# One 128x128 mask, `u` as a row, small fill matmuls, one unit's decay factors by DMA, and every order and bank anew in a RWKV-6 + FFN kernel

## The chip, the cores and the metric

The kernel runs on one core of a Trainium2 chip. The metric is the device time of one execution in microseconds (us); the median of 3 executions is given. TensorE is called PE, VectorE DVE, ScalarE ACT, GpSimd POOL and SyncE SP, as the profile does.

## The reference

Two parts follow each other. The first is a linear recurrence with a 48x48 state for each of 4 batches and 8 heads, over 768 steps; the second is four matrix products with one elementwise product among them.

```python
batch, n_heads, seq, head_dim = (4, 8, 768, 48)
n_tokens, d_model, d_ff = (3072, 384, 1024)
for t in range(S):
    cur = np.einsum('bhd,bhe->bhde', u[None] * kt, vt)
    y[:, :, t] = np.einsum('bhd,bhde->bhe', rt, state + cur)
    state = wt[:, :, :, None] * state + np.einsum('bhd,bhe->bhde', kt, vt)
x = y.transpose(0, 2, 1, 3).reshape(B * S, H * D)
a = x @ w1
b = x @ w2
h = a * b @ w3
return (h @ w_out).astype(np.float32)
```

All inputs and the output are float32; the matrix products of the kernel are in bfloat16.

## The kernel before

Time is cut into 6 chunks of 128 steps. A unit is one chunk of one batch (units 0 and 1) or of two batches (units 2 to 12), all 8 heads; there are 13 units. A step is named by its kind and its unit (`m_4_0`: unit 4, first of its two batches). Each unit has these steps.

- Loads `win`, `kin`, `rin`, `vin` (line 329; unit 0's `k`, `r`, `v` come as float32 into the tiles `wide`, line 320, and `kc`, `rc`, `vc` cast them, line 324).
- `ln` (402, ACT) is the logarithm of the decays; `cs` (414, PE) sums it over the chunk with the triangular matrix `LT`, and in the same step 4 matmuls of one column per batch (419) make the chunk's total decay, of which `pc` (426, ACT) takes the exponential. `ne`, `iw`, `e`, `et` (433, 472, 480, 457, ACT) are further exponentials; `KRk`, `rw`, `KRr`, `rk`, `ruk`, `dg`, `dv` (438, 476, 484, 518, 522, 528, 537) are the products with them, with `u` (tile `u_bc`) in `ruk`. `dv` holds the diagonal term.
- `k` and `r` are transposed on PE (`trk`, `trr`, `trw`, 510, 495, 463) and evicted (`trke`, `trre`, `KRw`), or by DMA on SP's queue (`dtk`, `dtr`, 504, 489).
- `m` (549, PE) is the 128x128 product within the chunk. It is masked to the strictly earlier steps: `msk` (568, DVE) multiplies it out of PSUM by the tile `mask`; where (unit, batch) stands in POOL_MASK, `mcp` (555, ACT) copies it and `maff` masks the copy, by a product (561, DVE) or an affine_select (563, POOL).
- `ys`, `yi` (584, 594, PE) form the output; `yb` (612, DVE) adds `dv`. For a unit in Y_PE, PE adds it (`yd`, 603) and ACT copies (`ybc`, 609). `yt` and `xT` (631, 635), or the DMA transpose `dty` (621), bring it into the layout of the FFN.
- `kv` (647, PE), `T` and `S` (655, 663) and `Sb` (668) carry the state to the next chunk.

The FFN: for each row block `fi` of w3, `wt` transposes it on PE (365), `w3Te` evicts it (369), `wm` multiplies it by w_out (374) and `w34e` evicts (379): so w3 and w_out become one matrix `w34`, whose product is done once. Then each unit has groups `a` and `b` (688, PE), `asb` (693, ACT), `abT` (698, DVE), the product `o` (704, PE), `osb` (709) and the store `st` (714, SP). The weights come in pieces: `w3_0` to `w3_3`, `wo`, and two halves each of w1 and w2.

`warm(at, n)` issues n matmuls of a tile of zeros (302) that nobody reads. They stand in the order where PE would have nothing else to do.

The order of all steps on all engines is written out by hand in `ORDER`, as name@engine; each engine runs its own steps strictly in that order and waits on semaphores for the others. SP, ACT and POOL also issue the DMAs that stand in their order: a DMA behind a waiting step waits too. `BANKS` gives each PSUM user its bank or banks, and each evicted tile its buffer (`sa`, `so`, `M`).

## Time and profile before

| | |
|---|---|
| median of 3 executions | 171.32 us (171.07 to 171.39) |
| the profiled execution: its own time | 171.16 us |
| the profiled execution: span of its instructions | 169.4 us |
| DVE, ACT and POOL busy | 134.1, 89.5 and 86.2 us |
| HBM read and written | 27.98 and 4.72 MB |

All times in rows are microseconds from the start of the span, unless marked ns. A row of a group reads: line, engine, operation, tiles out<-in, form, count | busy time, mean ns of one | idle time just before and what ended it. A matmul's own duration holds its passage through the array: matmuls follow each other faster than that. A row with a window gives, for each engine, its busy time in the window, then the granted clock of PE, and the DMA's share and rate.

```profile
DVE  0568889786789999999999999997799867556260
ACT  3166575258947789689855986611632042330511
POOL 7899874894773838994049607294072023000000
DMA  3999999999999999999959999959949944603313
```

These are 40 equal slices of the span, each with its busy share in tenths.

### The profile page before, as it was taken

The page shows a single profiled execution, that of the slowest core. Times are in us where ns is not written, and L with a number is a line of the kernel's source. Part 1 is how long each engine was busy: PE and PEld are TensorE (multiplying, and loading weights), DVE is VectorE, ACT ScalarE, POOL GpSimd, SP SyncE. Part 2 cuts the span into 40 slices and gives each one's busy share as a digit, 9 for nine tenths or more (in the row PEclk, how much of TensorE's full clock was granted, in tenths as well). Part 3 has the DMA queues.
Part 4 walks back from the last instruction along what each step waited for, and adds up shares of the span by engine and source line. Part 5 has one row for each costly group of instructions (what it writes and reads, how often), then busy time and mean ns, then how long its engine had stood idle before and what let it go on. Part 6 is the DMA issues. An engine that isn't in the chain of part 4 may idle for free.

```text
span 169.4 us, 4733 instructions
## 1 busy us (share of the span) xinstructions
PE 162.6 (96%) x1998; PEld 122.0 (72%) x1998; DVE 134.1 (79%) x221; ACT 89.5 (53%) x151; POOL 86.2 (51%) x83
## 2 busy tenths in 40 slices
...
DVE  0568889786789999999999999997799867556260
ACT  3166575258947789689855986611632042330511
POOL 7899874894773838994049607294072023000000
...
DMA  3999999999999999999959999959949944603313
GB/s 80 212 205 182 146 198 189 206 215 153 183 203 217 175 173 167 172 149 174 194 106 90 174 203 236 164 49 109 135 109 141 157 87 109 165 4 95 137 58 130
DMA packets 98837, 25.63 MB, mean 151 GB/s; under 512 B 90880, under 2 KB 96640, under 8 KB 98816
## 3 DMA queue, kind: packets, MB, share of 16 engines
...
HBM read 27.98 MB, written 4.72 MB: 193 GB/s over the span
## 4 chain that ended last, share of the span: by engine, by line
PE 73%; DVE 11%; DMA 7%; ACT 4%; issue 2%; POOL 1%; SPq 0%; DVEq 0%; ACTq 0%
PE banks L688 28%; PE banks L704 13%; PE banks L302 10%; PE banks L374 6%; DMA vin<-in_v_dram 5%; PE banks L549 3%; DVE abT L698 3%; PE banks L594 2%; PE banks L414 2%; PE banks L510 2%; PE banks L365 1%; DMA out_dram<-osb 1%; DVE dg L528 1%; ACT a_sb L693 1%; PE banks L647 1%
## 5 line engine op out<-in xcount | busy, mean ns | idle before, releaser
L688 PE MATMUL banks<-xT,w_bf 128*128 128x256 bf16 (+1 forms) x624 | 69.7, 264 | 0.5 <-DMA xT<-yb 0.4
L688 PEld LDWEIGHTS <-w_bf 128*128 128x128 bf16 x624 | 55.2, 98 | 7.8 <-issue 1.0
L693 ACT COPY a_sb<-banks 128x512 f32<-128x512 f32 x48 | 27.4, 594 | 27.8 <-PE banks L688 22.5
L698 DVE TENSOR_TENSOR abT<-a_sb,banks 128x512 bf16<-128x512 f32 x48 | 31.6, 681 | 10.4 <-PE banks L688 6.9
L704 PE MATMUL banks<-w,abT 128*128 128x384 bf16 x192 | 34.5, 326 | 0.1
L704 PEld LDWEIGHTS <-abT 128*128 128x128 bf16 x192 | 18.1, 98 | 10.7
L568 DVE TENSOR_TENSOR Mbf<-banks,mask 128x1024 bf16<-128x1024 f32 x17 | 20.4, 1219 | 1.6 <-PE banks L549 1.3
L302 PE MATMUL banks<-zeros 128*128 128x512 bf16 x66 | 19.9, 431 | 1.4 <-DVE zeros L243 1.3
L537 POOL TENSOR_TENSOR dv<-vin,dg 128x768 bf16<-128x768 bf16 x9 | 13.3, 1482 | 15.5 <-DMA vin<-in_v_dram 8.7
L709 ACT COPY osb<-banks 128x384 f32<-128x384 f32 x13 | 6.3, 482 | 21.7 <-PE banks L704 9.2
L329 POOL DMA_DIRECT2D win<-in_w_dram x13 | 15.0, 1157 | 1.1 <-POOLq L748 0.8
L329 POOL DMA_DIRECT2D rin<-in_r_dram x12 | 13.8, 1152 | 2.8 <-DMA w_bf<-in_moe_w_dram 2.5
L402 ACT ACTIVATE lw<-win 128x768 bf16<-128x768 f32 (+1 forms) x13 | 10.5, 811 | 8.7 <-DMA win<-in_w_dram 8.7
L329 POOL DMA_DIRECT2D vin<-in_v_dram x12 | 13.9, 1160 | 2.3 <-DMA w_bf<-in_moe_w_dram 0.9
L329 POOL DMA_DIRECT2D kin<-in_k_dram x12 | 13.8, 1153 | 1.7 <-issue 0.7
L612 DVE TENSOR_TENSOR yb<-banks,dv 128x768 bf16<-128x768 f32 (+1 forms) x12 | 11.1, 921 | 4.4 <-issue 1.8
L302 PEld LDWEIGHTS <-zeros 128*128 128x128 bf16 x66 | 6.5, 108 | 8.2 <-issue 3.8
L433 ACT ACTIVATE NEt<-banks 128x768 bf16<-128x768 f32 (+1 forms) x13 | 9.9, 765 | 3.6 <-PE banks L414 3.6
L663 POOL TENSOR_TENSOR Sst<-Tst,pc 128x384 f32<-128x384 f32 x4 | 3.7, 934 | 15.7 <-DVE Tst L655 15.6
L374 PE MATMUL banks<-wo_bf,w3T 128*128 128x384 bf16 x64 | 11.7, 325 | 0.0
L528 DVE TENSOR_REDUCE dg<-ruk 128x16 f32<-128x768 bf16 (+1 forms) x13 | 11.5, 881 | 0.0
L594 PEld LDWEIGHTS <-Mbf 128*128 128x128 bf16 x192 | 7.8, 96 | 2.5 <-issue 1.1
...
## 6 DMA issues: line engine op xcount, KB each, us to landing
out_dram<-osb SPq DMA_DIRECT2D x24, 192.0 KB, 2.1
win<-in_w_dram POOLq DMA_DIRECT2D x11, 384.0 KB, 9.8
kin<-in_k_dram POOLq DMA_DIRECT2D x11, 192.0 KB, 7.8
rin<-in_r_dram POOLq DMA_DIRECT2D x11, 192.0 KB, 8.4
vin<-in_v_dram POOLq DMA_DIRECT2D x11, 192.0 KB, 8.7
...
w_bf<-in_moe_w_dram POOLq DMA_DIRECT2D x4, 384.0 KB, 12.3
wo_bf<-in_moe_w_out_dram POOLq DMA_DIRECT2D x1, 768.0 KB, 13.5
```

Source lines behind the costliest of these rows:

```text
L302: nc.tensor.matmul(banks[:, at, :], lhsT=zeros[:, :C], rhs=zeros, start=True, stop=True)
L329: QUEUE[eng].dma_start(dst, src)
L374: nc.tensor.matmul(one(f"wm{fi}")[:, :DM], lhsT=w3T[fi % 2][:, gi, :], rhs=wo_bf[:, gi, :], start=(gi == 0), stop=(gi == FI - 1))
L528: nc.vector.reduce_sum(dgs, ruks, axis=AX.X)
L537: e.tensor_mul(dvs, vv, dgs[:, :, None].to_broadcast([C, bh, D]))
L568: nc.vector.tensor_mul(Mbf[bank[f"M{t}_{b}"]], mview(), mask.rearrange("s (j q) t -> s j q t", j=2))
L594: nc.tensor.matmul(o[:, h % 2, b, h // 2, :], lhsT=M[:, h % 2, h // 2, :], rhs=vv[:, b * H + h, :], start=(not c and b == 0 and h < 2), st ...
L612: nc.vector.tensor_add(ybs.rearrange("t b (q e d) -> t e (b q) d", e=2, d=D), yview().rearrange("t e (x d) -> t e x d", d=D), dvs.rearrang ...
L688: nc.tensor.matmul(o[:, f, :], lhsT=wt[:, di, fi * P:(fi + 1) * P], rhs=x[:, di, :T], start=(di == 0), stop=(di == DI - 1))
L693: copier(eng)(a_sb[bank[f"sa{t}_{g}"]], one(f"a{t}_{g}"))
L698: nc.vector.tensor_mul(ab[:, g * per:(g + 1) * per, :T], sa.rearrange("p (f t) -> p f t", t=T), one(f"b{t}_{g}").rearrange("p (f t) -> p f ...
L704: nc.tensor.matmul(one(f"o{t}_{b}")[:, :DM], lhsT=ab[:, fi, b * C:(b + 1) * C], rhs=w34[:, fi, :], start=(fi == 0), stop=(fi == FI - 1))
```

## The change

- `mask` becomes one 128x128 tile, `LT - I128` (DVE), which `msk` and `maff` read through a broadcast; its memset and its affine_select over 1024 columns go.
- `u` is loaded as one row of 384 numbers. One matmul with a row of ones (`ub`) spreads it over the partitions and ACT evicts it (`ue`).
- `warm` counts in quarters: n stands for n pieces of 128 columns, four of them to a matmul. The sum over all calls was 66 matmuls of 512 columns and is 144 pieces, so 36 such matmuls.
- The one-column matmuls become a step of their own (`cc`). Unit 10 has none: `px` (ACT) takes the exponential of the last rows of `cs`, and the DMA `pd` (SP) brings its last row to the partitions.
- `wide` and `u_f` lie inside the last two `abT` tiles; there are 4 `a_sb` buffers for 3.
- POOL_MASK has 4 members for 7, Y_PE has units 0 and 1. Unit 0's loads and `win_1` are issued by SP and ACT; before, `win_0` and `win_1` were POOL's.
- `ORDER` and `BANKS` are new throughout, engines included: `dv_6`, for one, goes to ACT, where it is 16 instructions, one for each of the unit's 2x8 head blocks.
- `DEPTH` is empty and `BLOCKS` has one unit each, so the code with them does what it did.

```diff
-N_X = 4
-N_ASB = 3
-N_AB = 8
+N_X = {2: 4}
+N_ASB = 4
+N_AB = {2: 8}
...
+DEPTH = {}
+BLOCKS = [(0,), (1,), (2,), (3,), (4,), (5,), (6,), (7,), (8,), (9,), (10,), (11,), (12,)]
+ROW_PC = {10}
...
-POOL_MASK = {(2, 0), (2, 1), (3, 0), (4, 0), (6, 1), (7, 1), (8, 1)}
-Y_PE = {1}
+POOL_MASK = {(2, 0), (4, 1), (7, 1), (9, 1)}
+Y_PE = {0, 1}
 BANKS = """
...
 ORDER = """
-table@ACT zeros@DVE u@SP win_0@POOL kin_0@SP rin_0@SP win_1@POOL vin_0@SP rin_1@POOL win_3@POOL kc_0@DVE padlw@DVE
-padet@DVE ones@DVE kin_1@POOL mask1@DVE LT@POOL win_2@POOL ln_0@ACT rc_0@DVE rk_0@DVE warm0@18 cs_0@PE padr@DVE
-kin_2@POOL padkr@DVE ln_1@ACT uc@ACT warm1@6 csT_1@PE w3_0@POOL pc_0@ACT cs_1@PE ruk_0@DVE et_1@ACT ne_0@ACT
-vin_1@POOL pc_1@ACT I128@POOL mask@POOL warm3@9 trw_1@PE csT_0@PE trw_0@PE ln_3@ACT kin_3@POOL ne_1@ACT warm4@3
-csT_3@PE KRk_1@DVE KRk_0@DVE rin_3@POOL rk_1@DVE warm6@2 trk_0@PE vc_0@DVE trk_1@PE KRw_1@DVE trke_0@ACT dg_0@DVE
-rin_2@POOL et_0@ACT et_3@ACT KRw_0@DVE ruk_1@DVE w3_1@POOL warm7@8 m_0_0@PE trke_1@DVE ln_2@ACT cs_3@PE msk_0_0@DVE
-wo@POOL kv_0@PE cs_2@PE vin_3@POOL m_1_0@PE pc_2@ACT ne_2@ACT msk_1_0@DVE warm4@2 wt_0_0@PE w3_2@POOL pc_3@ACT
-wt_1_0@PE ne_3@ACT wt_0_1@PE dg_1@DVE vin_2@POOL kv_1@PE csT_2@PE S_0@DVE dv_0@DVE yi_1_0@PE et_2@ACT dv_1@DVE
-win_4@POOL S_1@DVE warm7@3 yd_1@PE KRk_3@DVE ybc_1@ACT KRk_2@DVE warm7@2 trk_3@PE w3Te_0@ACT win_5@POOL Sb_0@DVE
-yt_1@PE yi_0_0@PE wt_1_1@PE Sb_1@ACT yb_0@DVE trw_3@PE w3Te_1@ACT trke_3@DVE w1_1@POOL warm1@1 trw_2@PE KRw_3@DVE
-trk_2@PE KRw_2@DVE warm4@1 m_3_1@PE rk_3@DVE warm7@1 m_3_0@PE trke_2@DVE mcp_3_0@ACT rin_4@POOL ruk_3@DVE warm7@4
-m_2_0@PE wt_2_0@PE maff_3_0@DVE mcp_2_0@ACT ys_3@PE wt_2_1@PE msk_3_1@DVE xT_1@ACT maff_2_0@POOL warm0@1 wt_3_0@PE
-warm1@1 wt_3_1@PE dg_3@DVE m_2_1@PE yt_0@PE mcp_2_1@ACT rk_2@DVE kin_4@POOL warm4@3 wm_0@PE ruk_2@DVE maff_2_1@POOL
-yi_3_0@PE w3Te_2@DVE wm_1@PE w34e_0@DVE dv_3@POOL dg_2@DVE yi_3_1@PE w3Te_3@ACT wm_2@PE rin_5@POOL yb_3@DVE w34e_1@ACT
...
-asb_8_1@ACT KRr_12@DVE o_7_0@PE KRk_11@DVE abT_8_0@DVE S_9@POOL dtk_11@SP T_10@DVE b_8_1@PE osb_7_0@ACT vin_12@POOL
-asb_9_0@ACT a_9_2@PE st_6_1@SP abT_8_1@DVE st_7_1@SP vin_11@POOL m_10_0@PE asb_9_2@ACT m_10_1@PE ys_10@PE msk_10_0@DVE
-a_9_1@PE S_10@POOL b_9_1@PE msk_10_1@DVE asb_9_1@ACT yi_10_0@PE b_9_2@PE abT_9_1@DVE yi_10_1@PE o_8_1@PE yb_10@DVE
...
+zeros@DVE kin_0@ACT win_0@SP padlw@DVE ones@DVE win_1@ACT u@SP padpx@DVE I128@POOL padkr@DVE table@ACT rin_0@SP
+padr@POOL vin_0@ACT win_2@POOL kc_0@DVE LT@POOL ln_0@ACT rin_1@POOL warm0@34 csT_0@PE cs_0@PE kin_1@POOL rc_0@DVE
+ne_0@ACT vin_1@POOL ln_1@ACT KRk_0@DVE uc@DVE et_0@ACT warm2@13 trk_0@PE mask@DVE win_3@POOL cs_1@PE vc_0@ACT warm4@3
+cc_1@PE csT_1@PE trw_0@PE cc_0@PE kin_3@POOL ln_2@ACT ne_1@ACT warm6@20 cs_2@PE kin_2@POOL et_1@ACT rk_1@DVE warm0@3
+cc_2@PE pc_1@ACT ub@PE KRk_1@DVE trw_1@PE rk_0@DVE ue@ACT trk_1@PE rin_2@POOL pc_0@ACT ne_2@ACT ruk_0@DVE trke_0@DVE
+padet@DVE KRw_1@DVE rin_3@POOL KRw_0@DVE ln_3@ACT warm0@29 m_0_0@PE w3_0@POOL kv_0@PE kv_1@PE msk_0_0@DVE trke_1@ACT
+w3_1@POOL warm2@6 csT_2@PE S_0@DVE m_1_0@PE et_2@ACT dg_0@DVE wo@POOL dv_0@DVE pc_2@ACT win_4@POOL ruk_1@DVE warm0@12
+csT_3@PE dg_1@DVE cs_3@PE KRk_2@DVE cc_3@PE vin_3@POOL msk_1_0@DVE pc_3@ACT trk_2@PE ne_3@ACT et_3@ACT vin_2@POOL
+rk_2@DVE trw_3@PE dv_1@DVE yi_1_0@PE trw_2@PE trke_2@DVE w3_2@POOL yi_0_0@PE yd_1@PE KRk_3@DVE yd_0@PE ybc_1@ACT
+win_5@POOL KRw_3@DVE ybc_0@ACT warm0@7 yt_1@PE trk_3@PE Sb_0@ACT KRw_2@DVE xT_1@ACT wt_1_0@PE rin_4@POOL trke_3@ACT
+S_1@DVE wt_1_1@PE ruk_2@DVE m_2_0@PE m_2_1@PE Sb_1@ACT mcp_2_0@ACT wt_0_0@PE msk_2_1@DVE wt_0_1@PE w1_1@POOL m_3_1@PE
+w3Te_0@ACT wt_2_0@PE msk_3_1@DVE yt_0@PE wt_2_1@PE xT_0@ACT m_3_0@PE w3Te_1@ACT maff_2_0@DVE warm2@1 ys_3@PE wt_3_0@PE
+dg_2@DVE wt_3_1@PE rk_3@DVE ruk_3@DVE kin_4@POOL warm7@16 wm_1@PE msk_3_0@DVE wm_0@PE w3Te_3@DVE ln_4@ACT rin_5@POOL
+dg_3@DVE w34e_1@ACT wm_3@PE iw_4@ACT w3Te_2@DVE w2_1@POOL w34e_0@DVE yi_3_0@PE dv_3@POOL w34e_3@ACT cs_4@PE yi_3_1@PE
+e_4@ACT yi_2_0@PE wm_2@PE ne_4@ACT dv_2@POOL yb_3@DVE yi_2_1@PE w34e_2@DVE kv_3@PE kv_2@PE kin_5@POOL yb_2@DVE
+wt_4_0@PE cc_4@PE wt_4_1@PE pc_4@ACT wt_5_0@PE w3Te_4@DVE yt_3@PE w1_0@POOL yt_2@PE xT_3@ACT S_2@DVE wt_5_1@PE wm_4@PE
+win_6@POOL w3Te_5@DVE ln_5@ACT Sb_2@ACT cs_5@PE rw_4@DVE w2_0@POOL wm_5@PE e_5@ACT T_3@DVE KRr_4@DVE xT_2@ACT S_3@DVE
+trr_4@PE iw_5@ACT w34e_4@DVE win_7@POOL cc_5@PE a_2_3@PE pc_5@ACT trre_4@ACT a_1_1@PE KRk_4@DVE vin_4@POOL a_2_2@PE
+w34e_5@ACT a_3_3@PE asb_2_2@ACT rw_5@DVE kin_6@POOL trk_4@PE ne_5@ACT KRr_5@DVE a_0_1@PE trke_4@ACT rk_4@DVE a_3_2@PE
...
+osb_1_0@ACT dv_7@POOL o_3_0@PE osb_2_0@DVE ln_10@ACT osb_0_0@ACT dv_6@ACT kv_6@PE m_6_0@PE T_6@DVE m_6_1@PE KRk_8@DVE
+a_5_2@PE msk_6_1@DVE b_4_1@PE a_5_3@PE msk_6_0@DVE b_5_1@PE asb_5_2@ACT b_5_3@PE S_6@DVE osb_3_0@ACT abT_5_1@DVE
+cs_10@PE asb_5_3@ACT a_4_2@PE st_3_0@SP st_1_0@SP px_10@ACT abT_5_3@DVE dtr_7@SP ys_6@PE kv_7@PE abT_4_1@DVE yi_6_0@PE
...
+o_2_1@PE Sb_6@DVE ne_10@ACT rk_9@DVE st_2_0@SP T_7@DVE pd_10@SP osb_3_1@ACT yt_6@PE st_0_0@SP abT_5_2@DVE asb_4_2@ACT
...
+b_7_3@PE rw_12@DVE asb_7_2@ACT rk_12@DVE o_6_0@PE KRr_12@DVE dty_8_1@SP osb_6_1@DVE dv_10@POOL a_9_3@PE abT_7_1@DVE
+dtk_10@SP a_9_2@PE abT_7_0@DVE vin_12@POOL osb_6_0@DVE a_9_0@PE asb_9_2@ACT dtr_11@SP abT_7_3@DVE a_8_1@PE asb_9_3@ACT
+vin_11@POOL ruk_12@DVE Sb_8@ACT a_8_3@PE abT_7_2@DVE asb_8_1@ACT st_6_1@SP st_5_1@SP b_8_1@PE rk_11@DVE asb_8_3@ACT
...
-    lw = many(N_A, [C, BH, PAD], BF, "lw")
+    lw = many(DEPTH.get("lw", N_A), [C, BH, PAD], BF, "lw")
...
+    prow = many(1, [P, P * NB * HP], F32, "prow")
...
-    mask = sb.tile([C, 2 * HP, C], BF, name="mask")
+    mask = sb.tile([C, C], BF, name="mask")
...
-    u_f = sb.tile([C, DM], F32, name="u_f")
-    wide = {(x, t): sb.tile([C, H, D], F32, name=f"wide_{x}{t}") for t in sorted(F32_IN) for x in "krv"}
+    late = [abT[2][i].rearrange("p f t -> p (f t)") for i in (N_AB[2] - 2, N_AB[2] - 1)]
+    u_r = late[0][0:1, 4 * DM:5 * DM]
+    late = [x.bitcast(F32) for x in late]
+    u_f = late[0][0:1, DM:2 * DM]
+    place = {"k": (1, 0), "r": (1, 1), "v": (0, 0)}
+    wide = {(x, t): late[i][:, j * DM:(j + 1) * DM].rearrange("p (h d) -> p h d", h=H)
+            for t in sorted(F32_IN) for x, (i, j) in place.items()}
...
-    @op("mask1")
-    def _(eng):
-        nc.vector.memset(mask, 1.0)
+    if ROW_PC:
+        @op("padpx")
+        def _(eng):
+            for x in prow:
+                nc.vector.memset(x[96:].rearrange("t (e d x) -> t e d x", e=2, d=PAD)[:, :, D:], 0.0)
 
     @op("mask")
     def _(eng):
-        nc.gpsimd.affine_select(mask, mask, compare_op=Alu.is_gt, fill=0.0, base=0, channel_multiplier=-1,
-                                pattern=[[0, 2 * HP], [1, C]])
+        nc.vector.tensor_sub(mask, LT, I128)
 
     @op("u")
     def _(eng):
-        nc.sync.dma_start(u_f, u.rearrange("h d -> (h d)").partition_broadcast(C))
+        QUEUE[eng].dma_start(u_f, u.rearrange("h d -> (h d)").rearrange("(p x) -> p x", p=1))
 
     @op("uc")
     def _(eng):
-        copier(eng)(u_bc, u_f)
+        copier(eng)(u_r, u_f)
+
+    @op("ub")
+    def _(eng):
+        nc.tensor.matmul(one("ub")[:, :DM], lhsT=LT[0:1, :], rhs=u_r, start=True, stop=True)
+
+    @op("ue")
+    def _(eng):
+        copier(eng)(u_bc, one("ub")[:, :DM])
 
     def warm(at, n):
-        for _ in range(n):
-            nc.tensor.matmul(banks[:, at, :], lhsT=zeros[:, :C], rhs=zeros, start=True, stop=True)
+        while n > 0:
+            k = min(n, 4) * C
+            nc.tensor.matmul(banks[:, at, :k], lhsT=zeros[:, :C], rhs=zeros[:, :k], start=True, stop=True)
+            n -= 4
...
-            if state:
+
+        if state and t not in ROW_PC:
+            @op(f"cc_{t}")
+            def _(eng):
                 o = col_view()
                 for b in range(nb):
                     for q in range(HP):
@@ -420,7 +451,18 @@
                                          lhsT=LW[:, b * H + 2 * q:b * H + 2 * q + 2, :].rearrange("t h d -> t (h d)"),
                                          rhs=ones_c, start=False, stop=True, skip_group_check=True)
 
-        if state:
+        if state and t in ROW_PC:
+            @op(f"px_{t}")
+            def _(eng):
+                dst = own(prow)[96:].rearrange("t (e d b q) -> t b q e d", e=2, b=nb, q=HP)
+                for b in range(nb):
+                    nc.scalar.activation(dst[:, b, :, :, :D], cs_view()[96:, b].rearrange("t (q e d) -> t q e d", e=2, d=D),
+                                         Act.Exp)
+
+            @op(f"pd_{t}")
+            def _(eng):
+                QUEUE[eng].dma_start(PC, own(prow)[C - 1:C])
+        elif state:
...
-                        nc.vector.tensor_mul(x, x, mask)
+                        nc.vector.tensor_mul(x, x, mask[:, None, :].to_broadcast([C, 2 * HP, C]))
...
-                    nc.vector.tensor_mul(Mbf[bank[f"M{t}_{b}"]], mview(), mask.rearrange("s (j q) t -> s j q t", j=2))
+                    nc.vector.tensor_mul(Mbf[bank[f"M{t}_{b}"]], mview(),
+                                         mask[:, None, None, :].to_broadcast([C, 2, HP, C]))
```

229 lines of the change are left out of this document (113 added, 116 removed).

## The prediction

> **What bounds the kernel now.** I read the first part of the page, then the windows of busy time, then single rows of the timeline.
>
> ```profile
> span 169.4 us, 4733 instructions
> PE 162.6 (96%) x1998; PEld 122.0 (72%) x1998; DVE 134.1 (79%) x221; ACT 89.5 (53%) x151; POOL 86.2 (51%) x83
> L302 PE MATMUL banks<-zeros 128*128 128x512 bf16 x66 | 19.9, 431 | 1.4 <-DVE zeros L243 1.3
> ```
>
> PE is idle for 169.4 - 162.6 = 6.8 us only. But 66 of its matmuls multiply zeros, so the page's 96% hides waiting. The windows show where; their cuts are the first fill, the first real matmul, the first `wm`, the first `a`, then later stretches:
>
> ```profile
> core 0: us, PE busy (x) PEld busy (x) DVE busy (x) ACT busy (x) POOL busy (x), PEclk, DMA share, GB/s
> 1.26:8.19 6.93, 6.93 (x19) 2.55 (x20) 2.18 (x9) 1.35 (x2) 6.11 (x7) 1.00 1.04 169
> 8.19:30.97 22.78, 22.55 (x286) 14.36 (x286) 19.20 (x40) 14.44 (x25) 18.40 (x20) 1.00 1.73 186
> 30.97:42.07 11.10, 11.10 (x124) 7.61 (x123) 7.95 (x14) 5.86 (x10) 8.52 (x9) 1.00 1.80 191
> 42.07:72.80 30.73, 30.73 (x498) 27.03 (x495) 28.21 (x47) 23.12 (x40) 21.44 (x19) 1.00 1.79 184
> 72.80:92.70 19.90, 19.72 (x253) 15.70 (x252) 19.65 (x33) 15.25 (x26) 11.04 (x11) 1.00 1.84 142
> 92.70:126.30 33.60, 33.60 (x418) 25.55 (x418) 30.77 (x47) 17.64 (x31) 15.55 (x13) 1.00 1.23 150
> 126.30:135.10 8.80, 7.90 (x126) 5.85 (x124) 8.58 (x11) 2.00 (x4) 2.00 (x3) 1.00 1.40 143
> 135.10:148.00 12.90, 12.45 (x144) 10.25 (x144) 8.11 (x13) 4.39 (x8) 2.95 (x2) 1.00 0.51 119
> 148.00:165.70 17.70, 17.67 (x148) 13.09 (x146) 9.21 (x14) 4.48 (x8) 0.00 (x0) 1.00 0.24 79
> 165.70:169.40 3.70, 0.00 (x0) 0.00 (x0) 0.00 (x0) 0.48 (x1) 0.00 (x0) 1.00 0.31 109
> ```
>
> From 30.97 on PE is the bound: its idle time there is 0.18 + 0.90 + 0.45 + 0.03 = 1.6 us, then 3.7 us of last eviction and store. Before 30.97 PE is not the bound, it fills. What it waits for at that point is in these rows, two of the timeline, one of the DMA view, and two more of the timeline:
>
> ```profile
> 1.26 6.93 PE L302 MATMUL banks<-zeros 128*128 128x512 bf16 x18 [1.26 <-DVE zeros L243]
> 16.72 0.94 POOL L348 DMA_DIRECT2D wo_bf<-in_moe_w_out_dram  x1
> wo_bf<-in_moe_w_out_dram POOLq DMA_DIRECT2D x1, 768.0 KB, 13.5
> 30.32 0.81 PE L302 MATMUL banks<-zeros 128*128 128x512 bf16 x3
> 30.97 1.46 PE L374 MATMUL banks<-wo_bf,w3T 128*128 128x384 bf16 x8
> ```
>
> w_out is issued at 16.72 and lands 13.5 us later, at 30.2; three fills end and the first `wm` starts at 30.97. The DMA row of the windows stays at 169 to 191 GB/s up to there, so the landing is set by the bytes queued ahead of it. The span thus is: first `wm` at 31.0, then 134.7 us of nearly dense PE to 165.7, then 3.7.
>
> **The change part by part.** *Fewer fills.* Leaving out a fill makes nothing arrive sooner. Up to the first `wm` there stand 65 fills: 18 in 6.93 us at the start, and 47 more. The pitch of the later ones is in the chain of waits, with two other rows for use below:
>
> ```profile
> 14.91 1.73 PE banks L302 x8
> ...
> 17.40 0.18 PE banks L419 x8
> ...
> 21.73 0.33 PE banks L603 x2
> ```
>
> 1.73 / 8 = 0.216 us, so 47 cost 10.2 us, and the real work ahead of the first `wm` is 22.55 - 10.2 = 12.4 us. Step by step, the new order has the same work ahead of its first `wm` (`wm_1`), and in addition `yd_0` (0.33, as `yd_1` in the row) and `ub` (one matmul, 0.16, half of that row): 0.5 us, 12.9 in all. Its fills ahead are all 144 pieces, 34 of them first: 34/4 x 0.385 (6.93/18) = 3.3 us, then 110/4 x 0.216 = 5.9 us. PE alone could thus start `wm_1` at 1.26 + 3.3 + 5.9 + 12.9 = 23.4 us. It cannot if w_out is not there.
>
> *What lands when.* Ahead of `wo` the new queues hold the same transfers as before (the loads of units 0 to 3 without `vin_2` and `vin_3`, then `w3_0` and `w3_1`) but for one, shown in the DMA view beside the load now first on its queue:
>
> ```profile
> u_f<-in_u_dram SPq DMA_DIRECT2D x1, 192.0 KB, 3.8
> wide_k<-in_k_dram SPq DMA_DIRECT2D x1, 192.0 KB, 4.4
> ```
>
> `u` over 128 partitions was 192 KB and becomes 1.5 KB: 0.197 MB / 186 GB/s = 1.06 us less ahead of everything. Three queues issue the first loads instead of two; at most this lifts the first window from 169 to 186 GB/s, 6.93 x 17 = 0.12 MB or 0.6 us; I take 0.4. So w_out lands at 30.2 - 1.06 - 0.4 = 28.7. The other engines allow that about: DVE was busy 0.27 + 2.18 + 19.20 = 21.7 us by 30.97, idle 9.3; by counting steps, the new order has 1.4 us less of DVE work ahead of `wm_1` (no memset of 1024 columns, `padr`, `vc`, `yb_0` and `maff` moved), which gives 29.6 if it idles as much, 28 if its first inputs come 1.5 us sooner. First `wm` at 28.8, bounds 23.4 (PE alone) and 31.0 (as before). Change: **-2.2 us**. Between 8 and 28.7 us PE then idles some 5 us openly where before it multiplied zeros; that is worth nothing either way.
>
> *After the first `wm`.* The next landing that PE meets is the first piece of w1, here from the timeline and the DMA view of its window:
>
> ```profile
> 23.97 0.75 POOL L340 DMA_DIRECT2D w_bf<-in_moe_w_dram  x1 [0.16 <-issue]
> w_bf<-in_moe_w_dram POOLq DMA_DIRECT2D x1, 384.0 KB, 16.3
> ```
>
> It landed at 40.3, for an `a` at 42.07. The new queue holds `rin_4` ahead of it (192 KB, 1.1 us) and lacks `u`: 40. The new first `a` has 12.3 us of PE work between it and `wm_1` by step counts (23.4 - 11.1): 28.8 + 12.3 = 41.1. It is met with 1 us to spare. Real work after `wm` loses `cc_10`'s 8 matmuls, by the row of 0.18: **-0.2**. The 66th fill, after 30.97, goes: **-0.2**.
>
> *The late wait for v.* `vin_11` and `vin_12` stood behind `S_9` and `S_10` on POOL.
>
> ```profile
> 135.09 0.36 PE L594 MATMUL banks<-vin,Mbf 128*128 128x48 bf16 x8 [0.89 <-DMA vin<-in_v_dram]
> ```
>
> Both are now issued right after `dv_10`, some 25 us of PE work ahead of unit 11's and 12's `yi`: **-0.9**.
>
> *Mask, and what moves between engines.* Rows by form:
>
> ```profile
> L568 DVE TENSOR_TENSOR Mbf<-banks,mask 128x1024 bf16<-128x1024 f32 x17 | 20.4, 1219 | 1.6 <-PE banks L549 1.3
> L555 ACT CAST Mbf<-banks 128x1024 bf16<-128x1024 f32 x7 | 7.1, 1013 | 3.1 <-PE banks L549 3.1
> L561 DVE TENSOR_TENSOR Mbf<-Mbf,mask 128x1024 bf16<-128x1024 bf16 x4 | 2.8, 704 | 0.1
> L522 DVE TENSOR_TENSOR ruk<-rk,u_bc 128x768 bf16<-128x768 bf16 x11 | 6.1, 557 | 0.1
> L518 DVE TENSOR_TENSOR rk<-rin,kin 128x768 bf16<-128x768 bf16 x11 | 6.0, 549 | 0.0
> ```
>
> A repeated operand costs nothing: `ruk` reads `u_bc` by a broadcast at 557 ns, `rk` reads plain tiles at 549. Three more `msk` (+3.6 us DVE) stand against three `maff` fewer on DVE (-2.1), five `xT` given to ACT (-2.8) and less preparation; DVE's sum falls by about 3 of 134 us. Covered by PE, except from 72.8 to 92.7, where DVE was busy 19.65 of 19.90 and the chain ran through it; there the new order asks DVE for about 4 us less ahead of the same PE step. I book nothing for it; without that cover it would be 1.5 us (3.6 - 2.1).
>
> *Decays of unit 10 by DMA.* `pd` moves 4 KB; the nearest row is a store:
>
> ```profile
> out_dram<-osb SPq DMA_DIRECT2D x24, 192.0 KB, 2.1
> ```
>
> SP waits in `pd` for `px` (two ACT instructions, counted below) with `st_0_0`, `st_3_1` and `dtk_9` behind it. But `px_10` stands three steps and more ahead on ACT, `S_10` needs the factors 40 us later, and unit 9's `m` comes some 15 us of PE later. Nothing; 2.1 us at most if unit 9 had to wait for it.
>
> *New stalls.* With every order new, some of the old 1.6 us returns elsewhere. The stalls left, 0.7 us, were those of the old plan; I book the same again: **+0.7**, bounds 0 and the third rival's.
>
> **Sum:** 169.4 - 2.2 - 0.2 - 0.2 - 0.9 + 0.7 = 166.6 us of span. The profiled execution took 171.16, 1.76 above its span, and the median is 0.16 above it: 166.6 + 1.76 + 0.16 = **168.5 us**.
>
> **Rivals.** *One, the head is shorter still.* If the three queues bring w_out by 27, PE's first `a` meets w1 instead, whose landing bounds it at 40 less 0.5: with 12.3 us before it, `wm` at 27.2, 1.6 us sooner: 166.9 us. For it: the old first window runs at only 169 GB/s. Against: DVE at 28 to 29.6.
>
> *Two, nothing gained in the head.* If the removed `u` was carried beside other transfers for free, w_out lands at 30.2 and only the late terms are left (-0.2 - 0.2 - 0.9 + 0.7): 171.3 - 0.6 = 170.7 us. For it: u's 3.8 us overlapped k's 4.4. Against: the rate is flat at 170 to 190 GB/s whatever is queued.
>
> *Three, ACT becomes the bound from the first `a` to `m_6_0`: slower.* ACT rows for this stretch:
>
> ```profile
> L693 ACT COPY a_sb<-banks 128x512 f32<-128x512 f32 x48 | 27.4, 594 | 27.8 <-PE banks L688 22.5 <-DVE abT L698 5.2
> L426 ACT ACTIVATE pc<-banks 128x8 f32<-128x8 f32 x9 | 1.6, 180 | 1.7 <-PE banks L419 1.7
> L668 ACT CAST Sbf<-Sst 128x192 bf16<-128x192 f32 x1 | 0.4, 366 | 0.0
> ```
>
> By counting steps with their rows' means, the old order gave ACT 31.3 us for 34.0 us of PE work in this stretch; the new one 40.4 for 38.0, with two more `ln`, one more `ne` and `w34e`, two `xT`, two `osb`, and `dv_6` in 16 pieces (`px` comes later). One piece of 48 columns lies between `pc`'s 180 ns (8 columns) and `Sb`'s 366 (192): 0.22 us, so 3.5 us in one block, with `asb_5_2`, `osb_3_0` and `asb_5_3` behind it and their PSUM banks held. Rows' means overlap, and busy time is about 0.9 of their sum: 36.4 of 38.0 us. Before, ACT idled 30.73 - 23.12 = 7.6 us in its stretch, waiting for PE. If as much waiting stays in the new order, the stretch lasts 36.4 + 7.6 = 44 us, +6.0: 174.5 us. It decides from 4.4 us of idle ACT: the first 1.6 cost nothing, 2.8 more take the gain. Against: much of that idle time was slack that a later PE leaves, and a fuller queue waits less.
>
> *Four, PE's speed in a head with holes.* 18 fills took 6.93 us at the start, 0.385 each; later ones 0.216. The head of before had no hole. If real holes kept PE at the first pitch, its 12.9 us of work become 23.0, 10.1 more against the 5.4 us of idle: +4.7, 173.2 us. Against: holes here are short, fills stand between them. The Trainium skill, TensorE: Matmul & The Clock Gate ("The HAM clock gate"), says that PE falls to half clock after an idle window of about 3.4 us. This speaks against leaving gaps; this trace shows the ramp, and no run here yet shows a fall.
>
> **How the numbers follow.** Forecast 0.52 (its own range 167.3 to 170.4: head 1.2 either way, new stalls up to 0.7 more); rival one 0.13, two 0.10, three 0.18, four 0.07. About 0.2% (0.34 us) is what can be told from no change, so 170.98 to 171.66 counts as the same. Faster: 0.50 + 0.13 + 0.06 + 0.02 = 0.71; same: 0.02 + 0.03 + 0.02 = 0.07; slower: 0.22 (most of three and four). The range runs from rival one, with 0.5 below it, into the lower parts of three and four, 166.4 to 172.8; it leaves out their upper parts and a little below, less than 0.2.
>
> **What would show it.** First `wm` near 28.8 with w_out's landing as what ended its wait, and open PE idle of about 5 us before it; the wait for v gone; PE idle from there to the last `o` about 1 us; the first `a` near 41. Rival three would show PE waiting for `a_sb` evictions between 41 and 79 us, ACT at 95%. It is wrong if `wm_1` starts at 25 or 31, or if PE's open idle after 45 us passes 3 us.

## The result and the profile after

| | before | after |
|---|---|---|
| median, same chip (4 executions each) | 171.28 us | 168.72 us |
| ratio, 95% interval | | 0.9857 (0.9833 to 0.9882) |
| the profiled execution | 171.16 us | 168.80 us |
| its span | 169.4 us | 167.1 us |

Faster by 1.4%; the forecast was 168.5 us. Run again on another chip (`after_again` below) the changed kernel was 1.0% faster than the kernel before. A ratio leaves out executions that took over 1.5% more than the shortest of their kernel, so it can lie below the quotient of the medians. Lines of the page after:

```profile
span 167.1 us, 4692 instructions
PE 156.5 (94%) x1964; PEld 119.5 (72%) x1967; DVE 131.6 (79%) x212; ACT 94.9 (57%) x173; POOL 81.7 (49%) x82
L326 PE MATMUL banks<-zeros 128*128 128x512 bf16 (+3 forms) x37 | 11.2, 415 | 1.4 <-DVE zeros L257 1.3
```

The fills fell from 19.9 to 11.2 us, PE's busy time by 6.1. Next the windows of busy time, cut at the end of the first fills, the first `wm`, the first `a`, and then by stretches (columns as before):

```profile
core 0: us, PE busy (x) PEld busy (x) DVE busy (x) ACT busy (x) POOL busy (x), PEclk, DMA share, GB/s
5.07:28.43 23.36, 19.29 (x269) 13.40 (x273) 18.16 (x37) 14.92 (x28) 17.50 (x18) 1.00 1.78 193
28.43:41.19 12.76, 12.63 (x169) 9.12 (x169) 10.34 (x17) 7.82 (x13) 10.75 (x10) 1.00 1.89 186
41.19:79.00 37.81, 37.75 (x533) 31.74 (x530) 32.43 (x50) 32.18 (x57) 29.96 (x27) 1.00 2.00 189
...
100.00:112.00 12.00, 11.20 (x177) 8.48 (x175) 10.27 (x15) 4.74 (x8) 7.15 (x7) 1.00 2.06 160
112.00:122.00 10.00, 9.37 (x99) 6.99 (x98) 9.56 (x15) 4.76 (x10) 3.96 (x3) 1.00 1.12 106
```

Three things are to be seen. Before the first `wm` PE is openly idle for 23.36 - 19.29 = 4.1 us, and the clock column stays at 1.00 all the same. From 41 to 79 us ACT is at 32.18 / 37.81 = 85%, and PE idles 0.06 us there. And the idle time that came back lies from 100 to 122: 0.80 + 0.63 us. The timeline of PE shows the landmarks:

```profile
28.43 4.06 PE L399 MATMUL banks<-wo_bf,w3T 128*128 128x384 bf16 x24 [0.81 <-DMA wo_bf<-in_moe_w_out_dram]
...
41.19 2.79 PE L729 MATMUL banks<-xT,w_bf 128*128 128x256 bf16 x30
...
101.40 0.43 PE L691 MATMUL banks<-vin,KR 128*64 128x48 bf16 x16 [0.80 <-DMA vin<-in_v_dram]
...
120.81 0.45 PEld L591 LDWEIGHTS <-KRT 64*128 64x128 bf16 x16 [0.50 <-DMA KRT<-KR]
```

The first `wm` moved from 30.97 to 28.43, and what ends its wait is w_out's landing, as forecast. The first `a` moved from 42.07 to 41.19. The wait for v at 135 is gone, and another one, of `kv_8`, stands at 101. By form, the mask and the moved `dv_6`:

```profile
L610 DVE TENSOR_TENSOR Mbf<-banks,mask 128x1024 bf16<-128x1024 f32 x20 | 24.0, 1219 | 2.9 <-PE banks L591 2.3 <-ACT KRT L556 0.4
L576 ACT ACTIVATE dv<-vin,dg 128x48 bf16<-128x48 bf16 x16 | 3.7, 360 | 0.0
```

`msk` takes 1219 ns with the broadcast tile, as it did with the wide one.

### The profile page after: what moved, and what is told of

Read it like the earlier page. It is cut to its first block, busy times and chain, and to the rows that moved or that the text cites. A ratio compares the mean times of both kernels' runs of the same rounds, so it can differ in the third digit from the quotient of the medians.

```text
span 167.1 us, 4692 instructions
## 1 busy us (share of the span) xinstructions
PE 156.5 (94%) x1964; PEld 119.5 (72%) x1967; DVE 131.6 (79%) x212; ACT 94.9 (57%) x173; POOL 81.7 (49%) x82
## 5 line engine op out<-in xcount | busy, mean ns | idle before, releaser
L739 DVE TENSOR_TENSOR abT<-a_sb,banks 128x512 bf16<-128x512 f32 x48 | 31.4, 679 | 4.5 <-ACT a_sb L734 2.3
L745 PE MATMUL banks<-w,abT 128*128 128x384 bf16 x192 | 33.8, 326 | 0.1
L610 DVE TENSOR_TENSOR Mbf<-banks,mask 128x1024 bf16<-128x1024 f32 x20 | 24.0, 1219 | 2.9 <-PE banks L591 2.3
L745 PEld LDWEIGHTS <-abT 128*128 128x128 bf16 x192 | 18.0, 97 | 11.2 <-issue 0.4
L579 POOL TENSOR_TENSOR dv<-vin,dg 128x768 bf16<-128x768 bf16 x8 | 11.9, 1498 | 15.0 <-DMA vin<-in_v_dram 9.7
L750 ACT COPY osb<-banks 128x384 f32<-128x384 f32 x14 | 6.8, 487 | 21.4 <-PE banks L745 13.1
L655 DVE TENSOR_TENSOR yb<-banks,dv 128x768 bf16<-128x768 f32 x11 | 10.4, 955 | 6.2 <-PE banks L637 2.5
L354 POOL DMA_DIRECT2D win<-in_w_dram x11 | 13.2, 1200 | 3.1 <-ACT a_sb L734 1.5
L326 PE MATMUL banks<-zeros 128*128 128x512 bf16 (+3 forms) x37 | 11.2, 415 | 1.4 <-DVE zeros L257 1.3
L560 DVE TENSOR_TENSOR rk<-rin,kin 128x768 bf16<-128x768 bf16 (+1 forms) x13 | 8.7, 667 | 2.0 <-DMA kin<-in_k_dram 2.0
L750 DVE COPY osb<-banks 128x384 f32<-128x384 f32 x10 | 5.5, 552 | 5.9 <-PE banks L745 3.0
```

The lines of the kernel that those rows point to most:

```text
L326: nc.tensor.matmul(banks[:, at, :k], lhsT=zeros[:, :C], rhs=zeros[:, :k], start=True, stop=True)
L354: QUEUE[eng].dma_start(dst, src)
L579: e.tensor_mul(dvs, vv, dgs[:, :, None].to_broadcast([C, bh, D]))
L610: nc.vector.tensor_mul(Mbf[bank[f"M{t}_{b}"]], mview(), mask[:, None, None, :].to_broadcast([C, 2, HP, C]))
L655: nc.vector.tensor_add(ybs.rearrange("t b (q e d) -> t e (b q) d", e=2, d=D), yview().rearrange("t e (x d) -> t e x d", d=D), dvs.rearrang ...
L739: nc.vector.tensor_mul(ab[:, g * per:(g + 1) * per, :], sa.rearrange("p (f t) -> p f t", t=n), one(f"b{ts[0]}_{g}").rearrange("p (f t) -> ...
```

## The experiments

Every kernel ran in five rounds beside the kernel before on its chip; ratios are to that. In those runs before had medians of 171.08 to 171.24 us.

### What u's row is worth

The kernel before with u as a row, `ub` and `ue` added and nothing else:

```diff
-    u_f = sb.tile([C, DM], F32, name="u_f")
+    u_f = sb.tile([1, DM], F32, name="u_f")
+    u_r = sb.tile([1, DM], BF, name="u_r")
-... cs_1@PE ruk_0@DVE ...
+... cs_1@PE ub@PE ue@ACT ruk_0@DVE ...
```

> The kernel before with u as a row and one matmul that spreads it; all fills stay. Landing theory: w_out lands 1.06 us sooner, at 29.1, but PE's own steps with the fills still end at 31, so the first wm stays at 31.0 to 31.2 and the time at 171.3 to 171.5 us. Theory that the 192 KB alone are the gain: 171.3 - 1.06 = 170.2 us.

170.26 us, ratio 0.9945 (0.9931 to 0.9959). And the changed kernel with u over 128 partitions again, `ub` and `ue` taken out:

```diff
-    u_f = late[0][0:1, DM:2 * DM]
+    u_f = late[0][:, DM:2 * DM]
-... pc_1@ACT ub@PE KRk_1@DVE ... rk_0@DVE ue@ACT trk_1@PE ...
+... pc_1@ACT KRk_1@DVE ... rk_0@DVE trk_1@PE ...
```

> The changed kernel with u loaded over 128 partitions again (192 KB), without ub and ue. Landing theory: w_out lands 1.06 us later than 28.39, first wm at 29.4, 168.7 + 1.0 = 169.7 us (ub's 0.16 saved is hidden in the wait). Theory that u's transfer is free: w_out at 28.4 and 168.6 us.

170.16 us, ratio 0.9941 (0.9922 to 0.9959). By the ratios this is 1.4 us above the changed kernel of the result (0.9857), and 0.8 above its second run (0.9897). Four of the six executions had a mean clock of 0.978 to 0.990, which none of the changed kernel had, so half clock may have a part in this median; the profiled one kept its clock. Its PE timeline and its row for w_out in the DMA view (median time from issue to landing last):

```profile
29.96 4.06 PE L391 MATMUL banks<-wo_bf,w3T 128*128 128x384 bf16 x24 [0.92 <-DMA wo_bf<-in_moe_w_out_dram]
...
42.35 2.80 PE L721 MATMUL banks<-xT,w_bf 128*128 128x256 bf16 x30
```

```profile
wo_bf<-in_moe_w_out_dram POOLq DMA_DIRECT2D x1, 768.0 KB, 15.6
```

w_out takes 15.6 us instead of 14.0, the first `wm` starts 1.53 us later and the first `a` 1.16 later. (In five profiled executions with the changed kernel's head the first `wm` starts between 28.14 and 28.54.) So u's 192 KB were not carried for free: that is rival two's condition, and it falls in both kernels. In the old order the same row was worth less, 0.9 us. The number is that of the second theory there, the way to it is not: w_out landed 0.9 us earlier, at 29.32, but the first `wm`, behind fills, moved only from 30.97 to 30.61 and the first `a` from 42.07 to 41.72. Of the 1.2 us between the profiled spans most of the rest came late: PE's wait ahead of `yi` at 135 us fell from 0.89 to 0.59, and one of 0.36 at 143 went. The landing theory had counted on no gain.

### Are the fills worth anything?

The kernel before with its first 18 fills alone, the 48 later ones taken out:

```diff
-                warm(int(name[4:]), int(eng))
+                if eng == "18":
+                    warm(int(name[4:]), int(eng))
```

> The kernel before without its 48 later fills (the first 18 stay). Landing theory (w_out's landing sets the first wm, fills are worth nothing): w_out still lands at 30.2 and the first wm starts there instead of at 30.97, so 171.3 - 0.7 = 170.6 us. Clock theory (holes in the head bring PE back to the slow pitch): the 12.4 us of work ahead of the first wm take up to 22 us, first wm up to 3 us later than 31, 171.5 to 174 us. Fill theory (the fills themselves were the loss): 10.2 us less, 161 us.

173.32 us (170.75 to 174.46), ratio 1.0049 (1.0017 to 1.0081). The windows of its profiled execution (174.33 us, one of the longest), cut where the clock changes:

```profile
10.21:13.62 3.41, 1.45 (x20) 1.20 (x20) 1.64 (x9) 2.01 (x5) 3.41 (x5) 1.00 1.60 182
13.62:27.27 13.65, 11.46 (x131) 9.55 (x130) 10.50 (x22) 7.95 (x13) 11.43 (x12) 0.50 1.83 180
```

The clock falls to half for 13.65 us after a stretch of 3.41 us in which PE was busy for 0.43 of the time. w_out lands at 29.48 there, 0.7 us earlier than before, but the first `wm` starts at 31.84. Over all executions the time goes with the clock: the three with a mean clock of 0.986 to 0.989 took 170.75 to 172.19 us, the nine with 0.956 to 0.970 took 171.95 to 174.46. The same with u's row in it, whose edits stand above:

> The kernel before with u as a row and without the 48 later fills. Landing theory: first wm at w_out's landing, 29.1 to 29.3, 1.8 us sooner: 169.5 us. Theory that u's transfer was carried for free: as without fills alone, 170.6 us. Clock theory: 171.5 to 174 us.

171.36 us, ratio 1.0011 (0.9987 to 1.0034): the half clock lasts one stretch of 3.41 us, and the first `wm` starts at 28.43, right at w_out's landing, 2.2 us earlier than with the fills. Yet the first `a` is at 41.57 against 41.72 with them. Why it is no earlier is shown in the next section. Next, the changed kernel with its first group of fills alone:

```diff
-                warm(int(name[4:]), int(eng))
+                if eng == "34":
+                    warm(int(name[4:]), int(eng))
```

> The changed kernel with only its first group of fills (all others taken out; nothing else touched). Clock theory: in the kernel before, taking the later fills out let the clock fall to half for 13.7 us and cost 2 us in the median; with w_out landing near 28.4 and the head's idle in PE rising from 4.1 us to about 8, the clock falls here too, for several microseconds at the least, the mean clock is below 0.99, wt and w3 come late, and the median is 169.5 to 172. Landing theory: w_out's landing alone sets the first wm, the fills are dead weight, the clock stays full, and the median stays at 168.5 to 168.8.

170.89 us, ratio 1.0003 (0.9983 to 1.0022). Its windows, cut at the clock's changes, and its PE timeline:

```profile
4.96:8.38 3.42, 1.68 (x27) 1.28 (x26) 1.12 (x4) 1.90 (x4) 3.42 (x4) 1.00 1.37 213
8.38:22.03 13.65, 10.02 (x116) 8.04 (x115) 9.95 (x23) 7.24 (x14) 12.53 (x14) 0.50 2.05 177
```

```profile
28.29 2.77 PE L399 MATMUL banks<-wo_bf,w3T 128*128 128x384 bf16 x16
...
41.35 2.80 PE L729 MATMUL banks<-xT,w_bf 128*128 128x256 bf16 x30
...
119.36 2.14 PE L729 MATMUL banks<-xT,w_bf 128*128 128x256 bf16 x18 [2.06 <-DMA xT<-yb]
```

The clock fell as the clock theory said, and the median rose as it said, but not where it said: the first `wm` starts at 28.29 and the first `a` at 41.35, against 28.43 and 41.19 with the fills. The slack ahead of w_out's landing took the whole of the half clock. Most of what this execution lost (2.5 us of span) it lost at 119 us, in a wait for a transpose by DMA, some 97 us after the clock had recovered; the changed kernel waits 0.38 us at that step. And two of the twelve executions kept a mean clock of 0.996 and still took 170.46 and 170.63 us, against 170.36 to 171.86 for the nine with 0.956 to 0.960. So the fills of the changed kernel hold its clock, but most of what its median gains from them is not the clock in the head; what it is stays open. A smaller cut, one group of four fills:

```diff
-... et_0@ACT warm2@13 trk_0@PE ...
+... et_0@ACT trk_0@PE ...
```

> The changed kernel without one group of four fills (0.87 us at 5.62), all others kept. Theory, that the clock is set by PE's busy share of stretches of about 3.4 us, with the fall near one half (stretches of 0.33, 0.41, 0.43 and 0.49 were followed by half clock, those of 0.52, 0.59 and 0.64 were not): the stretch that was at 0.59 in the changed kernel comes to 0.34, the clock falls in most executions for at least one stretch of 3.4 us, and the median is 169.3 to 171, with a wide scatter, as the stretches don't begin at the same time in each execution. Rival, that only a hole of a whole stretch or many holes in a row bring the fall: clock full, median 168.5 to 168.8.

169.41 us (169.04 to 170.36), ratio 0.9891 (0.9863 to 0.9918). On the same chip the unchanged version of this kernel took 169.68, so nothing was lost, though the number lies in the theory's range. In the profiled execution the clock stayed full: its stretches began elsewhere (the clock's first rise, which the column of the clock does not show, was at 6.48 us, not 5.46), and the hole was shared by two of them. Of the six executions five have a mean clock of 0.996 or more; one has 0.990, about what one stretch at half clock gives, and it was the shortest, 169.04 us. So the clock did not fall in most executions, as the theory had it, and where it may have fallen nothing was lost.

### Fills ahead of the first wm, and a collision of DVE and POOL

In the run with u's row and all fills, PE was still multiplying zeros when w_out had landed (at 29.32):

```profile
29.96 0.81 PE L311 MATMUL banks<-zeros 128*128 128x512 bf16 x3
30.61 1.46 PE L383 MATMUL banks<-wo_bf,w3T 128*128 128x384 bf16 x8
```

So the last nine of them ahead of the first `wm` were taken out of it:

```diff
-... rin_4@POOL ruk_3@DVE warm7@4
+... rin_4@POOL ruk_3@DVE
-... maff_2_0@POOL warm0@1 wt_3_0@PE
-warm1@1 wt_3_1@PE ... kin_4@POOL warm4@3 wm_0@PE ...
+... maff_2_0@POOL wt_3_0@PE
+wt_3_1@PE ... kin_4@POOL wm_0@PE ...
```

> The kernel before with u as a row (170.26 us median) and with the last nine fills ahead of the first wm taken out (2.2 us of PE time); mask, decay factors and the rest of the order as before. Theory, that in that kernel PE's own fills end after w_out has landed (first wm at 30.61, w_out at 29.32), so that the changed kernel's gain is u's row and the trimming of the fills together: the first wm starts at 28.4 to 29.4, the clock stays full, and the median is 168.9 to 169.4. Rival, that the other parts (the new order, the late wait for v, the shorter DVE work) carry the remaining 1.5 us: 170.0 to 170.4 as the head's gain is lost in the waits behind it.

171.39 us, ratio 1.0008 (0.9993 to 1.0023): 1.1 us slower than with the nine fills, and neither theory expected that. PE and DVE in the timeline of this run, then POOL:

```profile
29.50 1.46 PE L383 MATMUL banks<-wo_bf,w3T 128*128 128x384 bf16 x8
...
34.27 1.47 PE L383 MATMUL banks<-wo_bf,w3T 128*128 128x384 bf16 x8 [1.61 <-DVE w3T L378]
...
30.06 0.55 DVE L527 TENSOR_TENSOR rk<-rin,kin 128x768 bf16<-128x768 bf16 x1
30.64 2.97 DVE L531 TENSOR_TENSOR ruk<-rk,u_bc 128x768 bf16<-128x768 bf16 x1
33.53 0.68 DVE L378 COPY w3T<-banks 128x1024 bf16<-128x1024 bf16 x1
...
30.65 1.10 POOL L572 TENSOR_SCALAR_AFFINE_SELECT Mbf<-Mbf 128x1024 bf16<-128x1024 bf16 x1
31.71 1.48 POOL L546 TENSOR_TENSOR dv<-vin,dg 128x768 bf16<-128x768 bf16 x1
```

The first `wm` came 1.1 us earlier, as the theory said. But `ruk`, a product of two tiles in SBUF that takes 0.55 us, took 2.97 here: it began within 0.01 us of POOL's affine_select and did not end until POOL's `dv` behind that had ended, at 33.2. The eviction of w3's third block (`w3Te_2`) stands behind it on DVE, and PE waited 1.61 us for that. The first `a` came at 42.38 for 41.72, so 0.66 of the 1.2 us between the two spans is lost by then; the other 0.5 lies in waits from 135 us on (0.91 for 0.59, and one of 0.22 more). With the nine fills in place the same two engines stood so:

```profile
30.36 0.56 DVE L531 TENSOR_TENSOR ruk<-rk,u_bc 128x768 bf16<-128x768 bf16 x1
...
30.99 1.08 POOL L572 TENSOR_SCALAR_AFFINE_SELECT Mbf<-Mbf 128x1024 bf16<-128x1024 bf16 x1 [0.22 <-DVE ruk L531]
```

`ruk` was through in time, and POOL followed. In the two runs of this order without later fills `ruk` took 3.12 and 3.40 us at the same place, and PE waited 1.65 and 1.81 us for w3T; so part of what the first of them lost, and the 2 us between the first `wm` and the first `a` that the second gave back, are this collision and not the clock. The Trainium skill, SBUF — State Buffer ("SBUF: two separate sides"), says that DVE and GpSimd share a pair of ports as an exclusive lock, which an operation holds to its end while the other engine stands still. These rows agree, with 0.55 us against 2.97, except that the wait lasted over two operations of POOL.

The changed kernel has four members in POOL_MASK for seven, and from 24 to 44 us its POOL computes nothing but two `dv` (from 32.85 to 35.77); none of DVE's steps is drawn out there. That this is what lets the earlier `wm` pay is read from the rows and was not tried alone.

DVE steps are drawn out elsewhere, though. The unchanged version of this kernel ran once more beside the others:

> The changed kernel as it is, on the chip of these runs, to compare the versions with: 168.5 to 169.0, ratio to the kernel before 0.984 to 0.988.

169.68 us (168.91 to 170.07), ratio 0.9897 (0.9873 to 0.9922). This is above what was expected; the interval and that of the result, 0.9833 to 0.9882, just meet. Why is not known. The timelines of the first profiled execution and then of this one, the same lines of DVE and POOL, and one of PE:

```profile
71.62 1.18 DVE L560 TENSOR_TENSOR rk<-rin,kin 128x768 bf16<-128x768 bf16 x1
...
113.10 1.83 DVE L560 TENSOR_TENSOR rk<-rin,kin 128x768 bf16<-128x768 bf16 x1
...
72.26 1.23 POOL L707 TENSOR_TENSOR Sst<-Tst,pc 128x384 f32<-128x384 f32 x1
```

```profile
71.61 1.89 DVE L560 TENSOR_TENSOR rk<-rin,kin 128x768 bf16<-128x768 bf16 x1
...
114.07 1.83 DVE L560 TENSOR_TENSOR rk<-rin,kin 128x768 bf16<-128x768 bf16 x1
...
72.23 0.84 POOL L707 TENSOR_TENSOR Sst<-Tst,pc 128x384 f32<-128x384 f32 x1
...
75.94 0.81 PE L729 MATMUL banks<-xT,w_bf 128*128 128x256 bf16 x6 [0.41 <-DVE abT L739]
```

At 71.6 us this `rk` (0.55 us undisturbed) loses 0.6 us in one execution and 1.3 in the other. In the first it is POOL's `S` that is drawn out beside it, 1.23 us for 0.84; in the second `S` is through first and `rk` ends after it, and PE then waits 0.41 us at 75.9. That `S` is what holds `rk` up is not shown: undisturbed, `rk` would have ended at 72.17, before `S` began, and until then POOL was issuing a DMA (from 71.09 to 72.24 in the first), beside which the `rk` at 30.06 above kept its 0.55 us. The `rk` at 113 to 114 loses 1.3 us in both, and here a `dv` of POOL ran beside it (112.86 to 114.52 in the first). By 82 us the two executions stand 0.7 apart, of the 1.2 between their spans (167.1 and 168.3).

### w_out ahead of w3, and wm ahead of the transposes

```diff
-w3_1@POOL warm2@6 ... dg_0@DVE wo@POOL dv_0@DVE ...
+wo@POOL warm2@6 ... dg_0@DVE w3_1@POOL dv_0@DVE ...
-... wt_2_0@PE ... wt_2_1@PE ... wt_3_0@PE ... wt_3_1@PE ... warm7@16 wm_1@PE ... wm_0@PE ...
+... warm7@4 wm_0@PE ... wm_1@PE wt_3_0@PE wt_3_1@PE ... wt_2_0@PE wt_2_1@PE ...
```

With it `yi_3` and `cs_4` come to stand ahead of `wm_3`, and 13 pieces of fill go.

> The changed kernel with w_out's load put ahead of the second piece of w3 on POOL's queue, and wm_0 and wm_1 ahead of wt_3 and wt_2 on PE, 13 fills fewer. Landing theory: the first wm starts near 26 instead of 28.43, and as PE has then 2 us of transposes to do behind it, the head ends 0.6 to 1.2 us earlier: median 167.5 to 168.1. Rival, that the second piece of w3 and the first expert weights, which land later for it, end the head instead: the first wm is near 26 all the same, PE waits 2 us in what follows, and the median is 168.5 to 169.5.

169.53 us, ratio 0.991 (0.9894 to 0.9926). PE's timeline:

```profile
26.46 2.76 PE L399 MATMUL banks<-wo_bf,w3T 128*128 128x384 bf16 x16
...
31.48 0.56 PE L637 MATMUL banks<-vin,Mbf 128*128 128x48 bf16 x16 [1.36 <-DMA vin<-in_v_dram]
```

The first `wm` starts 2 us earlier, and the first `a` at 41.27 against 41.19. A wait for a load of v takes 1.36 us of it, and in all PE idles 12.76 - 11.40 = 1.4 us from 28.43 to 41.19 for 0.1 in the changed kernel. The rival was right that the gain is given back, but not by the loads it named: PE waits for v of unit 3, which lands at about 31.4 in both kernels. And the order has a share in it: `wm_3`, whose block of w3 was evicted by 30.47, stands behind that wait here and ahead of it in the changed kernel. Whether w_out's earlier landing would pay in another order was not tried.

### The waits that came back

PE's wait of 0.80 us at 101 is for the first of two loads that POOL issues behind `maff_7_1`. POOL's timeline in the changed kernel:

```profile
94.40 1.09 POOL L605 TENSOR_SCALAR_AFFINE_SELECT Mbf<-Mbf 128x1024 bf16<-128x1024 bf16 x1 [4.18 <-ACT Mbf L597]
95.44 2.36 POOL L354 DMA_DIRECT2D vin<-in_v_dram  x2
```

The loads of v for units 8 and 9, which stood behind `dv_7` and `maff_7_1` on POOL, moved up (the expectations below call a unit a head):

```diff
-... rin_10@POOL abT_3_1@DVE ...
+... rin_10@POOL vin_8@POOL vin_9@POOL abT_3_1@DVE ...
-vin_8@POOL yi_7_0@PE ... vin_9@POOL yi_7_1@PE ...
+yi_7_0@PE ... yi_7_1@PE ...
```

> The changed kernel with the loads of v for heads 8 and 9 moved on POOL's queue from behind dv_7 and maff_7_1 to right behind the load of r for head 10. Theory that the wait of kv_8 (0.80 us at 101.40, for a load issued at 95.44 behind maff_7_1) is on the path that sets the end: the wait is gone and the median is 167.8 to 168.1. Rival, that the chain behind it (the transposes and KR of heads 10 to 12) is late on its own account and PE waits there instead: 168.6 to 168.8, with the same idle time found a few microseconds later in the trace.

168.28 us, ratio 0.9847 (0.9828 to 0.9867). The wait at 101 is gone, and PE's idle time from 100 to 112 falls from 0.80 to 0.19 us; from 112 to 122 it grows from 0.63 to 0.85. The number lies between theory and rival, and by itself it cannot be told from the changed kernel of the result (0.9833 to 0.9882). Then the loads of v for units 12 and 11, put up behind that of unit 10:

```diff
-... vin_10@POOL KRr_11@DVE ...
+... vin_10@POOL vin_12@POOL vin_11@POOL KRr_11@DVE ...
-... vin_12@POOL osb_6_0@DVE ... vin_11@POOL ruk_12@DVE ...
+... osb_6_0@DVE ... ruk_12@DVE ...
```

> The changed kernel with the loads of v for heads 12 and 11 moved on POOL's queue to right behind that of head 10, so that they no longer fly beside the transpose of KR for head 10 (issued at 114.98, landed after 5.79 us). Theory that this load is held up by its neighbours: it lands in 4.5 us or less, PE's waits of 0.38 and 0.50 us after 117 go, and the median is 168.0 to 168.3. Rival, that its time is its own (many short descriptors): it takes over 5.3 us again and the median is 168.6 to 168.8.

170.90 us (169.00 to 172.14), ratio 0.9959 (0.9929 to 0.999), which neither theory had. The profiled execution took 172.07 us. In the DMA view from 105 to 120 us the last number of a row is the median from issue to landing: first the changed kernel, then this one.

```profile
xT<-yb SPq DMA_TRANSPOSE x4, 2.3
KRT<-KR SPq DMA_TRANSPOSE x3, 5.8
```

```profile
xT<-yb SPq DMA_TRANSPOSE x4, 4.9
KRT<-KR SPq DMA_TRANSPOSE x3, 3.4
```

KRT lands in 3.4 us, as the theory said: its 5.8 were those of the two loads beside it. But the loads of r and k for units 12 and 11 now stand behind those of v and fly beside the transposes of y instead, which take 4.9 us for 2.3. PE's timeline, and its windows round that wait:

```profile
117.31 5.76 PE L729 MATMUL banks<-xT,w_bf 128*128 128x256 bf16 x36 [2.01 <-DMA xT<-yb]
```

```profile
114.55:117.96 3.41, 1.40 (x11) 0.84 (x10) 2.85 (x6) 0.00 (x0) 0.60 (x1) 1.00 1.48 146
117.96:121.37 3.41, 3.41 (x18) 2.42 (x16) 3.38 (x7) 1.48 (x3) 0.00 (x0) 0.50 0.94 228
```

One hole of 2 us, in a stretch where PE was busy 0.41 of the time, also cost a stretch of 3.41 us at half clock, with 18 matmuls in it. Not every execution has it: six kept a mean clock of 0.996 or more and took 169.00 to 170.48 us; the six others, with 0.986 to 0.990, took 171.32 to 172.14. The last version puts all four loads of v early, but behind the other loads in line:

```diff
 ... rin_10@POOL vin_8@POOL vin_9@POOL abT_3_1@DVE ...
-kin_11@POOL m_9_1@PE ...
+kin_11@POOL vin_12@POOL vin_11@POOL m_9_1@PE ...
```

> The changed kernel with the loads of v for heads 8 and 9 behind r of head 10 as in the run of 168.28, and those for heads 12 and 11 behind k of head 11, where they are last in line and land before the transposes of y start. Theory, that the transpose of KR for head 10 is held up by these two loads (5.8 us beside them, 3.4 without): it lands in 4 us or less, PE's waits after 116 us go, and the median is 167.6 to 168.1. Rival, that the loads now collide with the transposes of y for heads 9 and 8 (as when they were put ahead of r of head 12): those land later than 1.3 us after their issue, PE waits for xT, and the median is 168.5 to 170.5.

168.50 us (168.13 to 168.73), ratio 0.9833 (0.9811 to 0.9854), beside 169.68 and 0.9897 (0.9873 to 0.9922) for the changed kernel on the same chip. The intervals do not touch, so on this chip it is faster than both kernels, by 1.7% and 0.7%. With the first ratio of the changed kernel, 0.9857 (0.9833 to 0.9882), its interval overlaps, so the 0.7% are less sure than the 1.7%. Its DMA view of the same window:

```profile
xT<-yb SPq DMA_TRANSPOSE x4, 2.6
KRT<-KR SPq DMA_TRANSPOSE x3, 3.8
```

The transposes of y are held up a little and KRT far less than before. PE's waits of 0.80 us at 101 and 0.50 at 121 fall to 0.20 and nothing; the one of 0.38 at 117 stays. It was forecast faster still, 167.6 to 168.1; its profiled execution lost 1.3 us in the `rk` at 71.6, as that of the unchanged version on this chip did.

## Why the prediction was right, point by point

- **The sum.** From the first `wm` to the end of the span the kernel took 138.4 us before and takes 138.7 now, where 0.6 less was forecast. So the whole net gain of 2.3 us is the head's. The sum came out because the head gave 0.3 us more than booked and the rest 0.8 less: the mechanism of the head was right, the closeness of the total is partly luck.
- **The head.** Forecast -2.2 us, measured 30.97 - 28.43 = 2.54. w_out landed at 28.39 for the 28.7 forecast, 1.8 us sooner than before; the other 0.7 is that no fills stand between the landing and the first `wm` any more. Inside it u's bytes were booked at 1.06 us by the DMA rate; taking them back moved w_out's landing by 1.5 here, and taking them out moved it by 0.9 in the old order. The rate of the windows priced the bytes too low for the new order and about right for the old one.
- **From the first `wm` to the first `a`:** 12.3 us were counted by steps (the counts behind its 23.4 and 11.1 are not shown), 12.76 measured, and the first `a` came at 41.19 for 41.1, as the first `wm` was 0.4 early. This held only because nothing stood in between. In the order before, an earlier `wm` was given back to the collision of `ruk` with POOL, which the prediction did not know of.
- **"Worth nothing either way"**, for the fills left out and the idle time in the head: right for `after`, where 4.1 us of open idle time cost no clock. As a general sentence it was wrong. In the kernel before, too few fills meant half clock, and the first `wm` started 2.4 us after w_out's landing (31.84 to 29.48).
- **Rival four** had a real mechanism with a wrong price and a wrong condition. It was priced at the first matmuls' pitch for all of the head's work; in the changed kernel without its later fills 13.65 us of half clock moved neither the first `wm` nor the first `a`. The Trainium skill, TensorE: Matmul & The Clock Gate ("The HAM clock gate"), has a free-running window of 3413 ns, and the changes of the clock in these traces lie 3.41 us or multiples of it apart. But no idle window was needed: shares of 0.41 and 0.43 (and 0.49 and 0.33 in two other runs) came ahead of a fall, and the longest hole in them was 2.0 us.
- **The late waits.** The wait for v went, -0.9, as said. The term that was mis-sized is "new stalls": 0.7 kept and 0.7 booked, 1.4 in all; by the windows 1.7 us of idle time lie between the first `wm` and PE's end. 0.80 of it is `kv_8`, behind a load issued at 95.44 behind `maff_7_1` on POOL: the very kind of wait that the change had removed at 135, made again at another place. The prediction looked up what was queued behind `pd` on SP, but not what was queued behind POOL's new `maff`.
- **Real work after the first `wm`** was to fall by 0.4 us. PE's busy time from there to its end is 133.3 us by the windows (to 163.40) for 133.2 before: nothing. Why was not found. The 0.5 that this is off, with 0.3 more of stalls and a head 0.3 shorter, are the 0.5 by which the span, 167.1, lies above the sum's 166.6.
- **Mask, decays, `dv_6`.** The broadcast costs nothing (1219 ns both times). `pd` landed 3.2 us after its issue, and nothing waited for it. `dv_6` took 3.7 us for the 3.5 booked.
- **Rival three** fell with one row: ACT at 85% from 41 to 79 us, not 95, and PE idle 0.06 us. The idle time of ACT was slack, as the counterargument had it.
- **Rivals one and two:** w_out did not land by 27, and when it was made to land at 25.4, the first `a` stayed where it was, at 41.27. Rival one's lower time was not there to be had by that landing alone, in the order that was tried.
